# A six-layer cross network: a second Strassen level for product 4 in both tiles, result blocks in an idle state tile, one more residual by DMA, and another order of weight loads

## The chip, the cores and the metric

The kernel runs on one core of a Trainium2 chip. Its metric is the device time of one execution in microseconds (us), lower is better. Three runs of the kernel before took 2219.45, 2219.56 and 2220.05 us; the median is 2219.56 us.

A core has five engines that run at the same time, each with its own queue in order. PE (TensorE) multiplies matrices and leaves the sums in PSUM banks. ACT (ScalarE) and DVE (VectorE) work element by element; here ACT brings PSUM banks to SBUF, and DVE adds and multiplies tiles within SBUF. POOL (GpSimd) and SP (SyncE) mostly issue transfers, which 16 DMA engines carry out.

## The reference

The batch has 16384 rows of 1024 features in bfloat16, and there are six layers:

```python
x = x0
for l in range(6):
    proj = einsum('bd,de->be', x, ws[l]) + bs[l]
    x = x0 * proj + x
return x
```

Each layer is thus one 16384x1024 by 1024x1024 product, a bias, an elementwise product with the first input, and a residual (adding the x from before the layer).

## The kernel before, in words

**Tiles and units.** The batch is cut into 16 tiles of 1024 rows (the code calls one a pair, `pr`), and two tiles make a group, of which there are eight. A *unit* is one layer of one tile; the kernel runs 96 units, within a group layer by layer: tile one (lane 0), then tile two (lane 1) of layer 0, then both of layer 1, and so on. So two neighbouring units use the same weights, and a unit's result is wanted by the unit after next. x is held transposed, features on partitions. There are three x0 tiles and three state tiles (`xst`); a group uses two of each, so one state tile is idle most of the time.

**Products.** A unit's 1024x1024 by 1024x1024 product is cut into 2x2 blocks of 512 and done with seven block products in place of eight (Strassen's method in Winograd's form). The code calls them 1 to 7. T1 to T4 are differences of x blocks, made by DVE: T1 = B12 - B11, T2 = B22 - T1, T3 = B22 - B12, T4 = B21 - T2. Weight sums 5, 6, 7 and 3 are made once in the first group and kept in DRAM. With bias, the four result blocks are Q = P1 + P2, U = P1 + P6 + P5 + P3, V = P1 + P6 + P7 + P5 and W = P1 + P6 + P7 + P4.

A block product on one level (function `group`, line 313) is four groups `P4.0` to `P4.3` of four 128x512 matmuls. With a second level (function `inner`, line 490) it is seven inner products, `4p1` to `4p7`, of four 128x256 matmuls each. Products 5, 2 and 3 have a second level in nearly all units. Product 4 has it where `K4` (line 152) names the lane: in both lanes in layer 0, and in lane 1 alone in layers 1 to 4. Seven units are plain, with one level throughout: the six of the first tile and the very last unit.

On one level product 4 is added into the PSUM banks in which P1, P6 and P7 already stand, and ACT brings the sum out with the bias (`E4.m`) as W. On two levels it has its own banks: DVE prepares `4t13`, `4t2`, `4t4` from T4, ACT moves seven pieces (`4e_...`, `4f1`, `4f2`), DVE adds `4cc`, and then `Wa` adds V to it while V is still P1 + P6 + P7.

**End of a unit.** DVE adds the parts (`Q1`, `Ua`, `Ub`, `Wa`, `Va`), multiplies each block by x0 (`Qm`, `Um`, `Vm`, `Wm`, line 560) and adds the residual. In layers 1 to 4 the residual of the blocks Q, U and V is an accumulating DMA issued by POOL (line 563, named `Qx`, `Ux`, `Vx`), and that of W is a DVE addition, `Wx`; `DMA_RES` (line 153) says which. Block W is at block row 2, column 1 ("block 21").

**Buffers.** The parts and results are in seven `ev` tiles. `NEXT` (line 176) says which tile takes over which part from one unit to the next, so that a tile read by a late instruction isn't written too early.

**Weights.** Weight blocks of 512 KB go through a ring of 12 SBUF slots. In groups two to eight a layer loads 10 or 11 of them in a fixed sequence (line 225; "5i" is the set of quarter sums of block 5). A load is issued on SP when the oldest slot's last use is issued (`pump`, line 239), so it goes to the slot of the load 12 places before it.

**Order.** PE's order within a unit is written out by hand: `PE_TWO` (line 25) where products 5, 2 and 3 have a second level, `PE_FOUR` (line 29) where product 4 has it too. The other engines' order comes from a planner (`schedule`, line 51): with planned durations it computes for each operation the latest time that keeps PE from waiting, and on each engine the ready operation with the earliest such time goes next. The order is then fixed. `ACCUM` (line 40) is the time from issue to landing that it plans for a residual DMA.

Of the kernel before, what the change touches and what calls it, by code (L numbers as in the profile page):

```python
# [9 lines left out]
ADD = mybir.AluOpType.add  # L10
# [12 lines left out]
P3.0 P4.3 P4.1 P4.0 P4.2  # L23
""".split()
PE_TWO = """
5p5 P1.1 5p1 P1.0 P1.3 5p2 2p5 5p6 2p1 P1.2 5p3 2p2 5p7 2p6 P6.0 5p4 2p3 3p5 2p7 3p1 P6.1 2p4 3p2 3p6 P6.2 P6.3 3p3
3p7 P7.0 P7.1 P7.2 3p4 P7.3 P4.1 P4.0 P4.3 P4.2
""".split()
PE_FOUR = """
5p5 P1.0 5p1 2p5 2p1 P1.1 5p2 5p6 2p2 P1.2 2p6 P1.3 5p3 5p7 2p3 2p7 P6.0 3p5 5p4 2p4 P6.1 P6.3 3p1 4p5 P6.2 4p1 3p2  # L30
P7.0 4p2 3p6 4p6 P7.1 3p3 4p3 4p7 P7.2 3p7 4p4 P7.3 3p4
""".split()
PE_LAST = """
P1.0 P1.1 P1.2 P1.3 P2.0 P2.1 P2.2 P2.3 P5.0 P5.1 P5.2 P5.3 P6.0 P6.1 P6.2 P6.3 P3.0 P3.1 P3.2 P3.3 P7.0 P7.1 P7.2 P7.3
# [2 lines left out]
ARRIVE = {"rows0": 4.9, "w0.1": 6.4, "rows1": 8.9, "rows2": 11.3, "w0.2": 11.9, "h0": 14.3, "h1": 15.5, "q": 17.5, "next": 21.0, "raw1": 40.0}  # L37


ACCUM = 9.0  # L40


class Op:
# [85 lines left out]
def kernel(  # L129
# [7 lines left out]
    nc = tc.nc  # L137
    P = nc.NUM_PARTITIONS
# [10 lines left out]
    KQ, HQ, NQ = KH // 2, H // 2, NB // 2  # L149
    RING = 12  # L150
    NDUMMY = 8
    K4 = {0: (0, 1), 1: (1,), 2: (1,), 3: (1,), 4: (1,)}
    DMA_RES = {1: "QUV", 2: "QUV", 3: "QUV", 4: "QUV"}

    const = ctx.enter_context(tc.tile_pool(name="const", bufs=1))
    dram = ctx.enter_context(tc.tile_pool(name="dram", bufs=1, space=bass.MemoryType.DRAM))
# [16 lines left out]
    ip["4"] = ip["2"]  # L173
    P1s, P5s, Q, U, V, W, C3 = (work.tile([P, KH, KH, P], BF16, name=f"ev{i}") for i in range(7))
    EV = {"5c": P5s, "3c": C3, "U": U, "V": V, "W": W, "Q": Q, "P1s": P1s}
    NEXT = {"5c": "3c", "3c": "5c", "U": "W", "V": "U", "W": "V", "Q": "Q", "P1s": "P1s"}
    home = {r: r for r in EV}
    TURNED, rows = ((0, 0), (1, 0), (0, 1)), (P1s, U, V)
    zeros = tin["4"][:, 0]
    ident = const.tile([P, P], BF16, name="ident")  # L180
# [40 lines left out]
    for gl in range(NGROUP * L):  # L221
        if gl < L:
            ring_seq += [(gl, w, "load") for w in RAW] + [(gl, w, "make") for w in MADE]
        else:
            ring_seq += [(gl, w, "load") for w in "1 5 5i 2 2i 6 3 3i 7 4 4i".split()[:11 if gl % L in K4 else 10]]
    slot = {(gl, w): f"slot{i % RING}" for i, (gl, w, _) in enumerate(ring_seq)}
    wt, uses_left, live = {}, {}, []
    pos = {"next": 0}
# [49 lines left out]
    for u, (pr, l) in enumerate(units):  # L278
        one, first, last = plain(u), u == 0, u == NU - 1
        if not first:  # L280
            home = {r: home[NEXT[r]] for r in home}
        P1s, P5s, Q, U, V, W, C3 = (EV[home[r]] for r in ("P1s", "5c", "Q", "U", "V", "W", "3c"))
        CB = {"5": P5s, "2": Q, "3": C3, "4": W}
        gl, grp, lane = gl_of(u), pr // 2, pr % 2
        x0T, xst = x0Ts[pr % 3], xsts[pr % 3]
        xs = x0T if l == 0 else xst
        X0 = {q: f"x0.{pr % 3}.{q[0]}{q[1]}" for q in QD}
# [25 lines left out]
        def group(name, w, bank, bname, rhs, rname, m, start, gl=gl, kmajor=kmajor):  # L313
            def fn():
                for k in range(KH):
                    r = rhs[:, k, :] if kmajor else rhs[:, :, k, :]
                    o = bank[:] if kmajor else bank[:].rearrange("p (j r) -> p j r", r=P)
                    nc.tensor.matmul(o, lhsT=wt[(gl, w)][:, k, m * P:(m + 1) * P], rhs=r,  # L318
                                     start=(start and k == 0), stop=(k == KH - 1), skip_group_check=True)
            if first and name in ("P5.0", "P5.1"):  # L320
                rname = rname + ["w0.5a"]
            else:
                rname = rname + wname(w)
            pe(name, 0.863, fn, rname, [bname], [w], at={"1": ARRIVE["w0.1"], "2": ARRIVE["w0.2"]}.get(w, 0.0) if first else 0.0)
# [25 lines left out]
        def fence(q, sp, u=u):  # L350
            def fn():
                nc.gpsimd.dma_start(seen[:], x0Ts[sp][0:1, q[1], q[0] * KH, 0:32])
            op(f"fence@{u}", "POOL", 0.6, 0.6, fn, [f"x0.{sp}.{q[0]}{q[1]}"], ["xbar"])

        if l == 0 and lane == 1:
            for q in QD:
# [119 lines left out]
        if not one:  # L476
            for X, a, b in (("5", 0, 1), ("2", 2, 3), ("3", 0, 1), ("4", 2, 3))[:len(inn)]:
                Bm, src = SRC[X]
                C, pn = CB[X], Pn[X]
                if kmajor:  # L480
                    q = lambda dh, n, k, Bm=Bm: Bm[:, dh * KQ + k, n * NQ:(n + 1) * NQ]
                    tk = lambda i, k, X=X: tin[X].rearrange("p i (k b) -> p i k b", k=KQ)[:, i, k]
                else:
                    q = lambda dh, n, k, Bm=Bm: Bm[:, n * KQ:(n + 1) * KQ, dh * KQ + k, :]
                    tk = lambda i, k, X=X: tin[X].rearrange("p i (j k r) -> p i j k r", j=KQ, k=KQ)[:, i, :, k, :]
                c = lambda dh, n, C=C: C[:, n * KQ:(n + 1) * KQ, dh * KQ:(dh + 1) * KQ, :].rearrange("p j m r -> p m j r")
                cn = lambda dh, n, pn=pn: [pn(2 * dh) + f".{n}", pn(2 * dh + 1) + f".{n}"]
                call = [pn(m) for m in range(KH)]

                def inner(i, bank, start, X=X, gl=gl, q=q, tk=tk, src=src, kmajor=kmajor):  # L490
                    quad = {1: (0, 0), 2: (1, 0), 3: (1, 1)}
                    rhs = (lambda k: q(*quad[i], k)) if i in quad else (lambda k: tk({4: 3, 5: 0, 6: 2, 7: 1}[i], k))
                    rn = {1: src, 2: src, 3: src, 4: X + "t4", 5: X + "t13", 6: X + "t2", 7: X + "t13"}[i]
                    w = X if i in (1, 2, 4) else X + "i"

                    def fn():
                        if i in (1, 2, 4):
                            k0, e0 = {1: (0, 0), 2: (KQ, 0), 4: (KQ, HQ)}[i]
                            wv = wt[(gl, w)][:, k0:k0 + KQ, e0:e0 + HQ]
                        else:  # L500
                            wi = weight(gl, w) if gl < L else weight(gl, w)[:]
                            wv = wi.rearrange("p q (k e) -> p q k e", k=KQ)[:, {5: 0, 6: 1, 3: 2, 7: 3}[i]]
                        for m in range(KQ):
                            for k in range(KQ):
                                o = pX[bank][:, m * NQ:(m + 1) * NQ]
                                nc.tensor.matmul(o if kmajor else o.rearrange("p (j r) -> p j r", r=P), lhsT=wv[:, k, m * P:(m + 1) * P],  # L506
                                                 rhs=rhs(k), start=(start and m == 0 and k == 0), stop=(k == KQ - 1), skip_group_check=True)
                    if gl < L and w.endswith("i"):
                        dep, wl = [f"is.{w}.{({5: '5', 6: '6', 3: '3', 7: '7'})[i]}", ISN[w]], []
                    else:  # L510
                        dep, wl = ([] if X in "24" else wname(w)), [w]
                    pe(X + f"p{i}", 0.436, fn, [rn, Xn[bank]] + dep, [Xn[bank]], wl)

                v3 = lambda bank: pX[bank][:].rearrange("p (m j r) -> p m j r", m=KQ, r=P)
                inner(5, b, True)
                copy(X + "e_p5", ip[X][:].rearrange("p j (m r) -> p m j r", r=P), v3(b), [Xn[b]], [("2" if X == "4" else X) + "ps"])
                inner(1, a, True)
                copy(X + "f1", pX[b][:], pX[a][:], [Xn[a]], [Xn[b]])
                inner(2, b, False)
                copy(X + "e_c11", c(0, 0), v3(b), [Xn[b]], call)  # L520
                inner(6, a, False)
                copy(X + "f2", pX[b][:], pX[a][:], [Xn[a]], [Xn[b]])
                inner(3, b, False)
                copy(X + "e_u0", c(0, 1), v3(b), [Xn[b]], call)
                inner(7, a, False)
                copy(X + "e_u1", c(1, 1), v3(a), [Xn[a]], call)
                inner(4, a, False)
                copy(X + "e_c21", c(1, 0), v3(a), [Xn[a]], call)
                ch = C[:, KQ:KH].rearrange("p j (d m) r -> p d j (m r)", d=2)
                ttop(X + "cc", ch, ch, ip[X][:].unsqueeze(1).to_broadcast([P, 2, KQ, KQ * P]), ADD, [("2" if X == "4" else X) + "ps"] + call, call, n=1024)  # L530
# [16 lines left out]
        if not last:  # L547
            if not one:
                ttop("Q1", Q[:], Q[:], P1s[:], ADD, allm("Q") + allm("P1s"), allm("Q"))
            ttop("Ua", U[:], U[:], P5s[:], ADD, allm("U") + allm("5c"), allm("U"))  # L550
            if not one:
                ttop("Ub", U[:], U[:], C3[:], ADD, allm("U") + allm("3c"), allm("U"))
            if "4" in inn:
                ttop("Wa", W[:], W[:], V[:], ADD, allm("W") + allm("V"), allm("W"))
            ttop("Va", V[:], V[:], P5s[:], ADD, allm("V") + allm("5c"), allm("V"))
            for nm, C, q in (("Q", Q, (0, 0)), ("U", U, (0, 1)), ("V", V, (1, 1)), ("W", W, (1, 0))):
                if l == 0:
# [148 lines left out]
        load_half("4", h)  # L706
    nc.sync.dma_start_transpose(out=blk(x0Ts[0], 1, 1), in_=x0[NB:2 * NB, H:2 * H])

    held = [i for i in order if ops[i].name.startswith("ld") and ops[i].name.endswith(".1@1")]
    for i in held:  # L710
        ops[i].fn()
    for i in order:
        if i not in held:
            ops[i].fn()
        for k in ops[i].weights:
            if k in uses_left:
                uses_left[k] -= 1
        pump()
# [30 lines left out]
```

## Time and profile before

| what | value |
|---|---|
| median of three runs | 2219.56 us |
| the profiled execution, whole | 2219.68 us |
| its span, first to last instruction | 2217.9 us |
| granted TensorE clock | 0.999 |
| PE busy | 2208.2 us (100% of the span) |
| DVE busy | 2144.3 us (97%) |
| ACT busy | 2037.4 us (92%) |
| POOL busy | 204.9 us (9%) |
| moved by DMA | 478.66 MB, mean 216 GB/s |

Busy time counts overlapping instructions once. Neighbouring instructions of DVE and of ACT overlap at their edges in the records, so a group's mean duration is longer than the distance at which such instructions follow each other: three DVE additions of 128x2048 that stand in one line of the timeline take 3.49 us together, though each is recorded with 1.22 us. The share of DMA is the mean share of busy time of 16 engines by the time of their packets, which overlap too, so it can be above 1 in a stretch.

### The profile page before, as it was taken

What the parts mean: (1) busy time and instruction counts of PE and PEld (TensorE: products, weight loads), DVE (VectorE), ACT (ScalarE), POOL (GpSimd) and SP (SyncE); (2) the same over time, 40 slices, a digit from 0 to 9 for tenths busy, and PEclk for the clock granted to TensorE, in tenths of its full rate; (3) what the DMA queues carried; (4) which work ended last, traced back from release to release, by engine and by line L of the source; (5) the groups of instructions that cost most, each with busy time, mean ns of one, the idle gap of its engine ahead of it and who ended that gap; (6) DMA issues with size and microseconds to landing.
All of it is one profiled execution on the core that took longest, in us unless ns stands there. A gap on an engine that the chain in (4) does not pass through costs nothing.

```text
span 2217.9 us, 39582 instructions
## 1 busy us (share of the span) xinstructions
PE 2208.2 (100%) x14625; PEld 1427.9 (64%) x14625; DVE 2144.3 (97%) x2527; ACT 2037.4 (92%) x3642; POOL 204.9 (9%) x263
## 2 busy tenths in 40 slices
PE   9999999999999999999999999999999999999998
PEld 5555566666666666666666666666666666666664
DVE  8999999999999999999999999999999999999997
ACT  7888899999999999999999999999999999999997
POOL 1122100110001100011000110011100111001110
PEclk9999999999999999999999999999999999999999
DMA  8777899768996689866898679986799877997777
GB/s 256 207 203 208 201 226 258 190 172 209 259 257 179 173 227 252 256 176 177 228 254 244 171 193 233 265 214 177 207 225 256 217 180 224 224 251 196 200 224 166
DMA packets 454306, 478.66 MB, mean 216 GB/s; under 512 B 269024, under 2 KB 381152, under 8 KB 454112
## 3 DMA queue, kind: packets, MB, share of 16 engines
q1 hardware_dynamic: 418352, 349.49, 53.8%
q0 software_dynamic: 35168, 126.38, 28.2%
q8 instruction: 114, 1.87, 0.3%
q14 instruction: 80, 0.66, 0.1%
q10 hardware_dynamic: 592, 0.27, 0.0%
HBM read 252.72 MB, written 58.20 MB: 140 GB/s over the span
## 4 chain that ended last, share of the span: by engine, by line
PE 98%; DMA 0%; DVE 0%; SPq 0%; issue 0%; POOLq 0%; ACT 0%; DVEq 0%; ACTq 0%
PE pA L318 52%; PE pX L506 43%; PE pX L318 3%; DMA wp<-in_ws_dram 0%; SPq L690 0%; DVE ev L204 0%; DMA xst<-x0T 0%; SPq L697 0%; DVE x0T L204 0%; DVE T L204 0%; POOLq L744 0%; ACT ev L337 0%; DVE x0T L421 0%; SPq L703 0%; SPq L700 0%
## 5 line engine op out<-in xcount | busy, mean ns | idle before, releaser
L506 PEld LDWEIGHTS <-wp 128*128 128x128 bf16 x8424 | 824.2, 98 | 272.3 <-issue 1.0
L337 ACT ACTIVATE ev<-pA,b_all 128x512 bf16<-128x512 f32 x1291 | 883.2, 691 | 114.2 <-PE pA L318 73.7
L318 PE MATMUL pA<-T,wp 128*128 128x512 bf16 x3856 | 924.0, 379 | 0.0
L318 PEld LDWEIGHTS <-wp 128*128 128x128 bf16 x5728 | 560.2, 98 | 493.8 <-issue 2.5
L327 ACT CAST ev<-pX 128x512 bf16<-128x512 f32 x1284 | 700.5, 596 | 22.5 <-PE pX L506 15.0
L506 PE MATMUL pX<-ti,wp 128*128 128x256 bf16 x4748 | 658.0, 273 | 0.0
L204 DVE TENSOR_TENSOR ev<-ev,ev 128x2048 bf16<-128x2048 bf16 x419 | 501.5, 1213 | 44.4 <-ACT ev L327 36.9
L204 DVE TENSOR_TENSOR ev<-ev,x0T 128x2048 bf16<-128x2048 bf16 (+1 forms) x324 | 383.9, 1204 | 1.0
L327 ACT COPY pX<-pX 128x512 f32<-128x512 f32 x628 | 364.6, 593 | 3.6
L318 PE MATMUL pA<-xst,wp 128*128 128x512 bf16 x1280 | 319.5, 379 | 0.0
L563 POOL DMA_DIRECT2D xst<-ev x192 | 166.0, 866 | 1294.6 <-ACT ev L337 491.9
L506 PE MATMUL pX<-xst,wp 128*128 128x256 bf16 x1736 | 260.4, 273 | 0.0
L506 PE MATMUL pX<-T,wp 128*128 128x256 bf16 x1588 | 238.2, 273 | 0.0
L204 DVE TENSOR_TENSOR ev<-ev,ip 128x1024 bf16<-128x1024 bf16 x314 | 209.2, 683 | 0.0
L204 DVE TENSOR_TENSOR T<-xst,T 128x2048 bf16<-128x2048 bf16 x160 | 194.8, 1217 | 2.5 <-PE pX L506 1.6
L204 DVE TENSOR_TENSOR T<-xst 128x2048 bf16<-128x2048 bf16 x160 | 194.8, 1217 | 0.1
L327 ACT CAST ip<-pX 128x512 bf16<-128x512 f32 x314 | 184.8, 589 | 0.4 <-PE pX L506 0.4
L204 DVE TENSOR_TENSOR xst<-ev,xst 128x2048 bf16<-128x2048 bf16 x124 | 150.7, 1217 | 0.0
L204 DVE TENSOR_TENSOR ti<-T,ti 128x512 bf16<-128x512 bf16 x272 | 113.4, 417 | 0.1
L204 DVE TENSOR_TENSOR ti<-xst 128x1024 bf16<-128x1024 bf16 x148 | 101.4, 685 | 8.3 <-PE pX L506 7.8
L204 DVE TENSOR_TENSOR ti<-xst,ti 128x1024 bf16<-128x1024 bf16 x148 | 101.2, 684 | 0.1
L204 DVE TENSOR_TENSOR ti<-T 128x1024 bf16<-128x1024 bf16 x136 | 92.9, 683 | 0.0
(57 smaller groups left out, 698.9 us busy)
## 6 DMA issues: line engine op xcount, KB each, us to landing
wp<-Lc SPq DMA_DIRECT2D x329, 512.0 KB, 6.1
xst<-ev POOLq DMA_DIRECT2D x192, 512.0 KB, 5.1
wp<-in_ws_dram SPq DMA_DIRECT2D x148, 512.0 KB, 6.8
out_dram<-x0T SPq DMA_DIRECT2D x60, 512.0 KB, 4.3
Lc<-wp POOLq DMA_DIRECT2D x24, 512.0 KB, 6.0
Lc<-xst POOLq DMA_DIRECT2D x23, 512.0 KB, 5.3
ev<-in_x_dram SPq DMA_DIRECT2D x3, 512.0 KB, 6.2
wp<-in_ws_dram SPq DMA_DIRECT2D x4, 256.0 KB, 7.5
```

Source lines behind the costliest of these rows:

```text
L204: nc.vector.tensor_tensor(out=o, in0=a, in1=b, op=op)
L318: nc.tensor.matmul(o, lhsT=wt[(gl, w)][:, k, m * P:(m + 1) * P], rhs=r, start=(start and k == 0), stop=(k == KH - 1), skip_group_check=True)
L327: act(name, lambda: nc.scalar.copy(out=dst, in_=src), rd, wr)
L337: act(name, lambda: nc.scalar.activation(out=dst, in_=src, func=IDENT, bias=b_all[:, c:c + 1], scale=1.0), rd, wr, True)
L506: nc.tensor.matmul(o if kmajor else o.rearrange("p (j r) -> p j r", r=P), lhsT=wv[:, k, m * P:(m + 1) * P], rhs=rhs(k), start=(start and m ...
L563: nc.gpsimd.dma_start(xblk(xst, *q), C[:], accum_op=ADD)
```

## The change

1. `K4` names both lanes in layers 0 to 4, so lane 0 of layers 1 to 4 has a second level in product 4 too and runs by `PE_FOUR` (except the plain first tile).
2. `DMA_RES` names W too: all four residuals of layers 1 to 4 are accumulating DMAs. `ACCUM` is 9.5 in place of 9.0.
3. In groups two to eight, lane 1 of layers 1 to 4 puts Q, U, V and W into the four blocks of the idle state tile (`S` names) and not into `ev` tiles. `NEXT` is another one, and a dependence without an instruction (`lend`) keeps the idle tile's other users apart from it.
4. Weight loads go in another sequence (`LOAD_ORDER`), and `PE_TWO` and `PE_FOUR` are other orders.
5. `Ua` is listed after `Wa` and not before `Ub`, which sets the order among additions that the planner rates alike.

The first loads of the second tile's x0, which the code sends ahead of everything else, are sent as before; only the list's name is another. `pump` is as it was.

```diff
 PE_TWO = """
-5p5 P1.1 5p1 P1.0 P1.3 5p2 2p5 5p6 2p1 P1.2 5p3 2p2 5p7 2p6 P6.0 5p4 2p3 3p5 2p7 3p1 P6.1 2p4 3p2 3p6 P6.2 P6.3 3p3
-3p7 P7.0 P7.1 P7.2 3p4 P7.3 P4.1 P4.0 P4.3 P4.2
+5p1 2p5 5p5 P1.1 P1.0 5p6 2p1 5p2 P1.2 P1.3 5p3 2p2 5p7 2p6 P6.0 3p5 5p4 2p7 2p3 P6.1 3p1 P6.2 2p4 3p6 3p2 P7.0 P7.1
+P6.3 3p3 P7.2 3p7 P7.3 P4.0 P4.1 P4.3 3p4 P4.2
 PE_FOUR = """
-5p5 P1.0 5p1 2p5 2p1 P1.1 5p2 5p6 2p2 P1.2 2p6 P1.3 5p3 5p7 2p3 2p7 P6.0 3p5 5p4 2p4 P6.1 P6.3 3p1 4p5 P6.2 4p1 3p2
-P7.0 4p2 3p6 4p6 P7.1 3p3 4p3 4p7 P7.2 3p7 4p4 P7.3 3p4
+P1.1 5p5 5p1 2p5 P1.3 P1.0 5p2 2p1 5p6 P1.2 2p2 2p6 5p3 5p7 P6.0 2p3 3p5 2p7 P6.3 5p4 2p4 P6.2 3p1 P6.1 4p5 3p2 4p1
+3p6 P7.0 4p2 4p6 3p3 P7.1 4p3 3p7 4p7 P7.2 3p4 4p4 P7.3
...
-ACCUM = 9.0
+ACCUM = 9.5
+LOAD_ORDER = "1 5i 2i 5 2 6 3i 3 4i 4 7".split()
...
-    K4 = {0: (0, 1), 1: (1,), 2: (1,), 3: (1,), 4: (1,)}
-    DMA_RES = {1: "QUV", 2: "QUV", 3: "QUV", 4: "QUV"}
+    K4 = {l: (0, 1) for l in range(L - 1)}
+    DMA_RES = {l: "QUVW" for l in range(1, L - 1)}
...
-    NEXT = {"5c": "3c", "3c": "5c", "U": "W", "V": "U", "W": "V", "Q": "Q", "P1s": "P1s"}
-    home = {r: r for r in EV}
+    NEXT = {"5c": "3c", "3c": "Q", "U": "U", "V": "W", "W": "V", "Q": "5c", "P1s": "P1s"}
+    cycle = {r: r for r in EV}
+    home = cycle
...
-            ring_seq += [(gl, w, "load") for w in "1 5 5i 2 2i 6 3 3i 7 4 4i".split()[:11 if gl % L in K4 else 10]]
+            ring_seq += [(gl, w, "load") for w in LOAD_ORDER if w != "4i" or gl % L in K4]
...
-            home = {r: home[NEXT[r]] for r in home}
+            cycle = {r: cycle[NEXT[r]] for r in cycle}
+        gl, grp, lane = gl_of(u), pr // 2, pr % 2
+        idle = (2 * grp + 2) % 3
+        home = dict(cycle)
+        if grp > 0 and lane and 0 < l < L - 1:
+            home.update({r: "S" + r for r in "QUVW"})
+        EV.update({"S" + r: xsts[idle][:, i // 2, i % 2] for i, r in enumerate("QUVW")})
...
+        if grp > 0 and lane == 0 and l in (1, L - 1):
+            op(f"lend@{u}", "POOL", 0.0, 0.0, lambda: None, (), [f"S{r}.{m}" for r in "QUVW" for m in range(KH)] + [f"xs.{idle}.{a}{b}" for a, b in QD])
...
-            ttop("Ua", U[:], U[:], P5s[:], ADD, allm("U") + allm("5c"), allm("U"))
             if not one:
                 ttop("Ub", U[:], U[:], C3[:], ADD, allm("U") + allm("3c"), allm("U"))
             if "4" in inn:
                 ttop("Wa", W[:], W[:], V[:], ADD, allm("W") + allm("V"), allm("W"))
+            ttop("Ua", U[:], U[:], P5s[:], ADD, allm("U") + allm("5c"), allm("U"))
             ttop("Va", V[:], V[:], P5s[:], ADD, allm("V") + allm("5c"), allm("V"))
```

More of the change, by code (lines that the diff above doesn't have):

```diff
@@ L280 @@
         if not first:
-            home = {r: home[NEXT[r]] for r in home}
+            cycle = {r: cycle[NEXT[r]] for r in cycle}
[5 more added lines that the diff above has]
+        EV.update({"S" + r: xsts[idle][:, i // 2, i % 2] for i, r in enumerate("QUVW")})
         P1s, P5s, Q, U, V, W, C3 = (EV[home[r]] for r in ("P1s", "5c", "Q", "U", "V", "W", "3c"))
         CB = {"5": P5s, "2": Q, "3": C3, "4": W}
-        gl, grp, lane = gl_of(u), pr // 2, pr % 2
         x0T, xst = x0Ts[pr % 3], xsts[pr % 3]
@@ L318, in fn @@
                     nc.tensor.matmul(o, lhsT=wt[(gl, w)][:, k, m * P:(m + 1) * P], rhs=r,
-                                     start=(start and k == 0), stop=(k == KH - 1), skip_group_check=True)
+                                                    start=(start and k == 0), stop=(k == KH - 1), skip_group_check=True)
             if first and name in ("P5.0", "P5.1"):
@@ L505, in fn @@
                                 o = pX[bank][:, m * NQ:(m + 1) * NQ]
-                                nc.tensor.matmul(o if kmajor else o.rearrange("p (j r) -> p j r", r=P), lhsT=wv[:, k, m * P:(m + 1) * P],
-                                                 rhs=rhs(k), start=(start and m == 0 and k == 0), stop=(k == KQ - 1), skip_group_check=True)
+                                nc.tensor.matmul(
+                                    o if kmajor else o.rearrange("p (j r) -> p j r", r=P), lhsT=wv[:, k, m * P:(m + 1) * P],
+                                    rhs=rhs(k), start=(start and m == 0 and k == 0), stop=(k == KQ - 1), skip_group_check=True)
                     if gl < L and w.endswith("i"):
@@ L707 @@
     nc.sync.dma_start_transpose(out=blk(x0Ts[0], 1, 1), in_=x0[NB:2 * NB, H:2 * H])
-    held = [i for i in order if ops[i].name.startswith("ld") and ops[i].name.endswith(".1@1")]
-    for i in held:
+    early = [i for i in order if ops[i].name.startswith("ld") and ops[i].name.endswith(".1@1")]
+    for i in early:
         ops[i].fn()
     for i in order:
-        if i not in held:
+        if i not in early:
             ops[i].fn()
```

## The prediction, made before the changed kernel ran

> **What bounds the kernel now.** I read the page first (engines, the chain that ended last, the DMA queues), then what PE waited for, then busy time unit by unit.
>
> ```profile
> PE 2208.2 (100%) x14625; PEld 1427.9 (64%) x14625; DVE 2144.3 (97%) x2527; ACT 2037.4 (92%) x3642; POOL 204.9 (9%) x263
> ...
> q0 software_dynamic: 35168, 126.38, 28.2%
> ...
> PE 98%; DMA 0%; DVE 0%; SPq 0%; issue 0%; POOLq 0%; ACT 0%; DVEq 0%; ACTq 0%
> ```
>
> PE is the bound, with DVE only 64 us of busy time behind. The view of waits, for PE:
>
> ```profile
> PE pX L681 <- DVE ti L678: 1.2, 1, 1.2
> PE pX L318 <- ACT pX L327: 0.7, 2, 0.5
> PE pX L318 <- DVE T L204: 0.6, 1, 0.6
> PE pX L417 <- DVE x0T L421: 0.4, 1, 0.4
> ```
>
> That is 2.9 us in all, so nothing but less PE work shortens the kernel. Next the busy times of stretches cut at unit borders of the fifth group: start and end, length, then PE, PEld, DVE, ACT, POOL, clock, DMA share, GB/s.
>
> ```profile
> 1135.60:1158.19 22.59, 22.59 (x163) 15.67 (x161) 22.59 (x29) 21.88 (x41) 0.00 (x0) 1.00 1.02 248
> 1158.19:1181.17 22.98, 22.98 (x151) 14.47 (x149) 22.98 (x28) 21.29 (x38) 1.42 (x2) 1.00 1.09 289
> ...
> 1249.33:1272.31 22.98, 22.98 (x151) 14.49 (x149) 21.72 (x26) 21.11 (x38) 2.59 (x3) 1.00 0.64 167
> 1272.31:1294.90 22.59, 22.59 (x162) 15.66 (x161) 22.14 (x28) 21.63 (x41) 2.59 (x3) 1.00 0.81 226
> ...
> 1363.45:1386.43 22.98, 22.98 (x150) 14.49 (x149) 22.98 (x27) 21.05 (x38) 0.00 (x0) 1.00 1.09 248
> ```
>
> Rows: layer 0 lane 1, layer 1 lane 0, layer 3 lanes 0 and 1, layer 5 lane 1. A unit costs PE 22.98 us with product 4 on one level, 22.59 on two. DVE is full from layer 5 through layer 1 lane 0, and PE goes on: a full DVE with work ready is borne. In layer 3 it idles 1.26 + 0.45 = 1.71 us a pair of units.
>
> **The gain on PE.** Lane 0 of layers 1 to 4 changes shape in seven groups (the first tile is plain): 28 units at 22.98 - 22.59 = 0.39 us, 10.9 us. It lies wholly on the path that sets the end. The chain in order of time gives the same from its pieces (start, length, matmuls):
>
> ```profile
> 1255.55 1.75 PE pX L506 x16
> ...
> 1268.14 4.32 PE pA L318 x20
> ```
>
> Product 4 on one level is 16 matmuls at 4.32 / 20, 3.46 us; on two, 28 at 1.75 / 16, 3.06 us. A group of four is 0.864, an inner product 0.437.
>
> **DVE.** Distances come from the timeline:
>
> ```profile
> 1254.54 3.49 DVE L204 TENSOR_TENSOR ev<-ev,x0T 128x2048 bf16<-128x2048 bf16 x3
> ```
>
> Less the last one's 1.22 us, 128x2048 operations start 1.14 apart; by the starts, 128x1024 ones are 0.60 apart, 128x512 ones 0.33. Lane 0 gains `4t13` 0.60, `4t2` and `4t4` 0.33 each, `4cc` 0.60, `Wa` 1.14: 3.00 us. Both lanes lose `Wx`, 2.28 a pair. A pair goes from 43.86 busy (21.72 + 22.14) to 44.58, while PE goes from 45.57 to 45.18: spare time falls from 1.71 to 0.60. Over the kernel: 28 x 3.00 - 64 x 1.14 = +11 us, DVE 2155. Layer 0 has this shape in both lanes already, DVE full, and PE didn't stop. I cost it at nothing but for one place. Its cover is those 0.60 us; every further us of idle that the order forces on DVE in a pair lengthens 28 pairs.
>
> **The one place: T2 in lane 0.** In the changed order of DVE the border from lane 1 to lane 0 in layers 2 to 4 reads 3cc, 4cc, Ub, Wa, 3t13, Ua, 23t2, Va, T2; T2 stands behind Va, and `P6.0` needs T2. Counted from the new unit's start: the old unit ends with P7.2, 3p4, 4p4, P7.3 so P7.2 ends at -1.74. ACT takes it up some 0.20 later (a group issued from 1267.98 on, over at 1268.84, is evicted from 1269.04), then the two copies 0.59 and 0.49 further on: -0.95 and -0.46. These rows give the step from ACT to a waiting DVE:
>
> ```profile
> 1262.22 1.10 ACT L327 CAST ev<-pX 128x512 bf16<-128x512 f32 x2
> ...
> 1263.36 1.23 DVE L204 TENSOR_TENSOR ev<-ev,ev 128x2048 bf16<-128x2048 bf16 x1 [1.26 <-ACT ev L327]
> ```
>
> The second cast starts near 1262.73 and DVE at 1263.36: 0.63. So 3cc starts at -0.32, 4cc at 0.28, Ub 0.88, Wa 2.02, 3t13 3.16, Ua 3.76, 23t2 4.90, Va 5.50, T2 6.64; T2 is out at 7.86, or 7.91 with the 0.04 to 0.05 of such a hand-over. In PE's new order four groups and ten inner products stand ahead of `P6.0`: 7.83. PE would wait 0.03 to 0.08, say 0.07, in 20 units (three a group, two in the first that has them): 1.4 us. From both sides: nothing if a hand-over is 0.1 shorter, 8 us if the chain comes 0.4 later in each. I take 1.4, since all its steps have rows here. Other users have room: T2 of lane 1 stands ahead of Ua, 23t2 is done 0.9 before 2p6.
>
> **ACT.** Four biased evictions (0.59 apart) become seven copies (0.48): about +1 us in lane 0, so 21.11 becomes the 21.65 of today's lane 1, in 22.59. Layer 0 runs two such units in a row without a wait. Nothing.
>
> **POOL and the fourth residual.** 64 more issues of 0.86 us: POOL goes from 2.59 to 3.45 us a unit, queueing only more residuals and, in the first group, saves of weight sums. There, 8 more DMAs stand between saves, and DVE is 1.14 a unit shorter; PE has no wait, so no gain: nothing. The landing matters: `2t13` of the unit after next needs W, and DVE is queued behind it. DVE work between a block's multiplication and its next reader, by the distances above: U 9.3 and 10.4 us (behind lane 1 and lane 0), W 9.1 and 9.9, V about 10, Q more. Landings of this transfer in the whole run, least, median, most:
>
> ```profile
> DMA to landing us min/median/max: 4.5/5.1/9.5
> ```
>
> In layer 3 the most is 5.0 in the lane-0 stretch and 7.7 in the lane-1 stretch. Queue q0 is 28.2% of 2217.9 us, 625 us of all engines, for 239 transfers of 512 KB: 2.6 us each. One more a unit raises the share by 0.115: 0.64 to 0.75, 0.81 to 0.93, still below the 1.02 to 1.09 of layers 5 to 1, where weights land in 8.6 at the most. Bounds for the longest landing: 5.0 and 9.5; I take 8.5 for the lane-1 stretch (nearest row 7.7 at 0.81), under its 9.9. Nothing.
>
> POOL's issues here take 852 to 1191 ns, median 862, beside a DVE that is 97% busy; none was held for the length of a DVE operation. A rule of the Trainium skill speaks against the step all the same: SBUF — State Buffer, "SBUF: two separate sides", has it that POOL can't write the descriptors of its DMAs while DVE runs an operation in a two-port performance mode. By that rule each issue could wait for the end of a DVE operation, 1.22 us, and a landing of 8.5 would become 9.7, just under the 9.9: the sum stays, and the room is gone.
>
> **Buffers and weights.** Lane 1 writes its blocks to the idle state tile, which the previous group's outputs leave during layer 0; its first writer is lane 1 of layer 1, over 20 us later. Elsewhere `NEXT` makes 2's first result wait for Va of lane 1: Va is out at 6.72, the result could leave its bank at 6.71. That is a wait of ACT's, and the next inner product that needs the bank, 2p3, starts at 8.69: nothing. Weight loads: from the last use of a slot's old block to the first use of the new one the least is 12.6 us in the new order (block 5, into layer 5) against 9.6 before (3i); landings have a median of 6.4 and a worst of 11.6. The order of loads is worth nothing, in either direction.
>
> **The sum.** Against the profiled execution: 2219.68 - 10.9 + 1.4 = 2210.2 us; the median of the three runs is 0.12 lower, so 2210.1.
>
> **Rivals.**
> 1. *Small waits eat part of it.* DVE's or ACT's late operations hold PE a further 0.1 to 0.3 us a pair: 28 x 0.1 to 0.3 = 3 to 8 us on top of the sum, so 2213 to 2218.5. For: the first unit of layer 0 (1386.43 to 1409.17) is 22.74 long, not 22.59, without a releaser shown. Against: 2.9 us of waits today.
> 2. *DVE becomes the bound* (the other side). If the 1.71 us of idle in a pair are forced by the order and stay, a pair takes 44.58 + 1.71 = 46.29, against 45.57 before: +0.72 x 28 = 20 us, 2240. It decides from 45.57 - 44.58 = 0.99 us of forced idle on. For: 1.26 of it is a wait for ACT at one place in lane 0. Against: that unit is the light one, and DVE has no idle at all over the four full units. By my own chain 0.5 us a unit before 3cc is left, which is about the spare time and no more.
> 3. *The fourth residual lands late*, by rising traffic or because DVE holds up POOL's issues. DVE then waits in `2t13` or T1. A wait up to 0.60 us a pair is free; from 0.99 on, a landing of some 10.9 us in lane 1's stretch, it is slower than before; 12 us would give 2.1 a pair: (44.58 + 2.1 - 45.57) x 28 = +31, 2251. Against: 7.7 now, and issues of at most 1.19 us. The second of the two ways is the rule of that page, SBUF — State Buffer, in the Trainium skill.
>
> **How the numbers follow.** Three runs lie within 0.03%; I call 0.2%, 4.4 us, the least that can be told from no change: faster is below 2215.1, slower above 2224.0. Forecast 0.62, its own range 2207.6 to 2213 (layer 0's 0.15 us waits gone as well and no T2 wait, up to twice the T2 wait and a little more). Rival 1: 0.14, 0.06 of it faster. Rival 2: 0.14, 0.02 of it within 0.2%. Rival 3: 0.10, slower (0.08 by traffic, 0.02 by held issues). Faster 0.62 + 0.06 = 0.68, same 0.08 + 0.02 = 0.10, slower 0.12 + 0.10 = 0.22. The range takes the forecast, rival 1 and the mild end of rival 2: 2207.6 to 2224, some 0.8.
>
> **What would show it.** Right: lane 0 of layers 2 to 4 takes 22.6 to 22.7 us, PE's waits stay under 5 us and name T or DVE, DVE is some 2155 busy, 256 residuals land in under 9. Wrong: PE's waits come to tens of us in layers 1 to 4, DVE idle there names ACT (rival 2) or the residual's DMA (rival 3).

## The result, and the profile after

The changed kernel takes 2283.25 us (median of five runs, 2282.85 to 2284.88); the kernel before, run beside it, 2220.05 us. The ratio is 1.0288 with a 95% interval of 1.0277 to 1.0299: 63 us slower, where 10 us faster was forecast. The profiled execution has a span of 2281.5 us, against 2217.9 before.

The page of the kernel after, its busy times, its queue of accumulating DMAs (packets, MB, share of the 16 engines) and its chain that ended last:

```profile
PE 2209.3 (97%) x14913; PEld 1459.7 (64%) x14961; DVE 2165.2 (95%) x2603; ACT 2054.4 (90%) x3726; POOL 256.6 (11%) x327
...
q0 software_dynamic: 44384, 159.94, 34.1%
...
PE 41%; DVE 37%; DMA 14%; issue 6%; ACT 1%; SPq 0%; DVEq 0%; POOLq 0%; ACTq 0%
```

PE was 98% of the chain before; now DVE and DMA have half of it, though DVE's busy time is only 10 us above the forecast (2165 against 2155). The view of waits, for PE and then for DVE (total us, times, longest us):

```profile
PE pX L516 <- ACT pX L334: 23.7, 29, 2.1
PE pA L325 <- DVE T L206: 13.3, 17, 0.8
PE pX L516 <- DVE ti L206: 10.6, 13, 1.2
```

```profile
DVE ti L206 <- DMA xst<-ev: 40.9, 27, 4.6
DVE ti L206 <- DMA x0T<-in_x_dram: 16.8, 6, 4.1
DVE ev L206 <- ACT ev L344: 12.0, 10, 2.6
```

PE's waits went from 2.9 to over 50 us, and name ACT and DVE. By place, the row for `T` is T2 in front of `P6.0`, and the row for `ti` is `23t2` in front of `2p6`; all but one of these 30 waits stand in lane 0 of layers 2 to 4. Of the 23.7 us for ACT, 21 stand in the first unit of layer 0 and the first of layer 5. But DVE itself waits 40.9 us for residuals (`xst<-ev`; line 574 now) and 16.8 us for loads of the next group's x0. The landing times of the residuals say why; least, median, most, in the kernel after:

```profile
DMA to landing us min/median/max: 4.5/6.6/13.0
```

The most was 9.5 before. Where the time went, from the distances between the first evictions of P1 in neighbouring units (a unit of this shape takes 22.59 us of PE work; where the order of products ahead of that eviction has changed, its 0.44 us are taken out):

| place | us |
|---|---|
| 28 units with less PE work | -10.9 |
| lane 0 of layers 2 to 4 (22.59 to 26.56 each), seven groups | +34.5 |
| first unit of layer 0 (25.60 to 26.05 in place of 22.74), six groups | +19.4 |
| from lane 1 of layer 4 to the next group, six groups | +11.5 |
| last units and tail | +7.0 |
| first group | +1.8 |
| the rest of layers 0 and 1 | +0.4 |
| sum | +63.7 |

Lane 1 of layers 1 to 3 takes exactly 22.59 everywhere. So most of the loss has two addresses: lane 0 in the middle layers, and the border from layer 4 into the next group.

**Lane 0 in the middle layers.** Windows of the kernel after cut at unit borders of the fifth group (columns as in the prediction): layer 2 lane 1, layer 3 lanes 0 and 1.

```profile
1253.49:1276.08 22.59, 22.59 (x162) 15.66 (x161) 19.64 (x22) 21.76 (x40) 3.44 (x4) 1.00 0.72 187
1276.08:1301.82 25.74, 23.23 (x162) 15.63 (x161) 25.24 (x33) 21.83 (x40) 3.44 (x4) 1.00 0.88 225
1301.82:1324.41 22.59, 22.59 (x162) 15.65 (x161) 20.48 (x24) 21.76 (x41) 3.44 (x4) 1.00 0.71 186
```

DVE idles about 3 us at the end of the lane-1 stretch, and the lane-0 unit is 3.15 longer. The timeline of DVE at that border (start, length, operation, and in brackets the idle time before it and what ended it):

```profile
1276.30 0.69 DVE L206 TENSOR_TENSOR ti<-xst 128x1024 bf16<-128x1024 bf16 x1 [3.04 <-DMA xst<-ev]
...
1278.98 1.22 DVE L206 TENSOR_TENSOR xst<-xst,ev 128x2048 bf16<-128x2048 bf16 x1
1280.11 1.22 DVE L206 TENSOR_TENSOR xst<-xst 128x2048 bf16<-128x2048 bf16 x1
1281.25 0.68 DVE L206 TENSOR_TENSOR ti<-xst 128x1024 bf16<-128x1024 bf16 x1
...
1283.59 1.22 DVE L206 TENSOR_TENSOR xst<-xst,ev 128x2048 bf16<-128x2048 bf16 x1
1284.72 1.22 DVE L206 TENSOR_TENSOR T<-xst,T 128x2048 bf16<-128x2048 bf16 x1
```

The first row is `2t13`, which stood 3.04 us for W's residual. Behind it, in order, come 3cc and 4cc (left out), Ub, Wa, `3t13`, Ua and 23t2 (left out), Va, T2: the border that the prediction wrote down, but all of it late. The chain in order of time goes on from T2 (start, us, what):

```profile
1268.53 11.49 DMA xst<-ev
...
1284.72 1.23 DVE T L206
1285.95 0.04 issue
1285.99 1.02 PE pA L325 x4
```

PE's `P6.0` starts 0.04 after T2. The 11.49 us piece is V's residual, which lands at 1280.01. `3t13` reads it at 1281.25 and doesn't wait, since W's wait has put it back already; 3.04 earlier it would have stood 1.8 us for V. In the pair before, `3t13` stood 1.33 us for V.

**What else moved.** The DMAs of this lane-1 stretch, by time from its first eviction of P1, set beside the same stretch of the kernel before:

| | before | after |
|---|---|---|
| weight loads | 11, issued from 5.64 to 22.07 | 11, issued from 5.20 to 21.77 |
| residuals near them (time issued, us to landing) | U 3.84, 8.0; Q 14.29, 6.8 | U 7.82, 7.9; W 10.09, 12.6; V 15.03, 11.5; Q 18.37, 12.0 |
| these transfers of 512 KB, and time until all have landed | 13 in 25.0 us | 15 in 30.7 us |
| lane 0's V | issued at 2.01, landed after 4.9 | as above |

U, W and V are lane 0's, Q is lane 1's. So not one but two residuals joined the loads here: W, which was a DVE addition, and V, which was sent 3.6 us ahead of the first load and is now sent 9.8 us behind it. The loads are issued over the same length of time. Over lane 1 of layers 2 and 3 in groups two to eight, the 13 transfers take 24.7 to 27.0 us before, the 15 take 28.5 to 31.4 after.

The mean share of DMA over such a unit hides the burst. The stretch for which the prediction read 0.81 (layer 3 lane 1 before), cut where U is issued:

```profile
1272.31:1277.65 5.34, 5.34 (x40) 3.81 (x39) 5.34 (x7) 4.96 (x10) 0.87 (x2) 1.00 0.11 21
1277.65:1294.90 17.25, 17.25 (x124) 11.85 (x122) 16.80 (x22) 16.67 (x32) 1.72 (x2) 1.00 1.03 290
```

It is 0.11 for 5 us and 1.03 for 17. So in its burst the kernel before already had a share as high as in the layers with the highest (1.02 to 1.09).

### The profile page after: what moved, and what is told of

It reads as the page before. It is cut to its first block, busy times and chain, and to the rows that moved or that the text cites. A ratio compares the mean times of both kernels' runs of the same rounds, so it can differ in the third digit from the quotient of the medians.

```text
span 2281.5 us, 40476 instructions
## 1 busy us (share of the span) xinstructions
PE 2209.3 (97%) x14913; PEld 1459.7 (64%) x14961; DVE 2165.2 (95%) x2603; ACT 2054.4 (90%) x3726; POOL 256.6 (11%) x327
## 4 chain that ended last, share of the span: by engine, by line
PE 41%; DVE 37%; DMA 14%; issue 6%; ACT 1%; SPq 0%; DVEq 0%; POOLq 0%; ACTq 0%
PE pA L325 21%; PE pX L516 18%; DVE ev L206 14%; DMA xst<-ev 12%; DVE ti L206 9%; DVE T L206 8%; DVE xst L206 6%; PE pX L325 2%; DMA x0T<-in_x_dram 1%; DMA wp<-Lc 0%; DVE wp L206 0%; ACT ev L344 0%; ACT pX L334 0%; DMA xst<-x0T 0%; SPq L701 0%
## 5 line engine op out<-in xcount | busy, mean ns | idle before, releaser
L325 PE MATMUL pA<-T,wp 128*128 128x512 bf16 x3377 | 851.7, 380 | 15.0 <-DVE T L206 13.3
L516 PE MATMUL pX<-ti,wp 128*128 128x256 bf16 x5196 | 725.1, 273 | 16.0 <-DVE ti L206 10.6
L344 ACT ACTIVATE ev<-pA,b_all 128x512 bf16<-128x512 f32 x955 | 649.6, 691 | 83.9 <-PE pA L325 46.6
L206 DVE TENSOR_TENSOR ev<-ev,ev 128x2048 bf16<-128x2048 bf16 (+1 forms) x307 | 367.6, 1219 | 12.7 <-ACT ev L344 12.0
L516 PE MATMUL pX<-T,wp 128*128 128x256 bf16 x1924 | 289.1, 273 | 8.0 <-ACT pX L334 7.8
L206 DVE TENSOR_TENSOR ev<-ev,x0T 128x2048 bf16<-128x2048 bf16 (+1 forms) x212 | 253.5, 1204 | 1.1
L574 POOL DMA_DIRECT2D xst<-ev x144 | 124.3, 863 | 759.9 <-ACT ev L334 412.2
L344 ACT ACTIVATE xst<-pA,b_all 128x512 bf16<-128x512 f32 x224 | 154.7, 691 | 9.4
L574 POOL DMA_DIRECT2D xst<-xst x112 | 96.2, 859 | 571.7 <-ACT ev L334 356.3
L206 DVE TENSOR_TENSOR ti<-xst 128x1024 bf16<-128x1024 bf16 x148 | 102.1, 691 | 46.1 <-DMA xst<-ev 40.9
L206 DVE TENSOR_TENSOR xst<-xst,x0T 128x2048 bf16<-128x2048 bf16 x112 | 136.9, 1223 | 0.7
```

The source lines that it names most:

```text
L206: nc.vector.tensor_tensor(out=o, in0=a, in1=b, op=op)
L344: act(name, lambda: nc.scalar.activation(out=dst, in_=src, func=IDENT, bias=b_all[:, c:c + 1], scale=1.0), rd, wr, True)
L574: nc.gpsimd.dma_start(xblk(xst, *q), C[:], accum_op=ADD)
```

## The experiments

My theory A: the residuals land late because too many transfers meet in lane 1's stretch, and DVE's wait for them delays PE through T2 and `23t2`. Its rival B: DVE's order and its load (prediction's rival 2) are the bound, and the DMA waits only show where DVE's idle time falls. For the border of groups, theory C: layer 4 as changed sends V too late, and the x0 loads hang behind it.

**All residuals a quarter of the size.**

```diff
-nc.gpsimd.dma_start(xblk(xst, *q), C[:], accum_op=ADD)
+nc.gpsimd.dma_start(xblk(xst, *q)[:, 0:1], C[:, 0:1], accum_op=ADD)
```

> The changed kernel with every residual DMA of layers 1 to 4 cut to a quarter of its block (one of four row tiles, 128 KB in place of 512); three quarters of those residuals are left out, all orders and waits stay. Theory A (residuals that land late behind the weight loads of lane 1 hold DVE, and that holds PE): landings under 6 us, lane 0 of layers 2 to 4 back to 22.6 us each, and the time falls by the 30 us or so that these units cost, to 2235 to 2255 if the first unit of layer 0 stays long (its x0 loads come late for another reason) and to 2210 to 2215 if it goes too. Theory B (the order of DVE and ACT itself forces idle, whatever the DMAs do): the waits stay, 2270 or more.

2239.79 us, ratio 1.0088 (1.0072 to 1.0105): 43 us of the 63 are gone. Lane 0 of layers 1 to 4 takes 22.59 to 22.62 in groups two to eight, the first unit of layer 0 still 25.80 to 26.05 from the third group on. The waits of DVE in this kernel:

```profile
DVE ti L206 <- DMA x0T<-in_x_dram: 18.0, 7, 4.8
DVE ev L206 <- ACT ev L344: 15.1, 10, 3.7
```

No row names a residual, and its DVE does the same work in the same order. B is refuted, A holds, and the wait for x0 is a matter of its own.

**W's residual alone a quarter of the size.**

```diff
-nc.gpsimd.dma_start(xblk(xst, *q), C[:], accum_op=ADD)
+p = slice(0, 1 if nm == "W" else KH)
+nc.gpsimd.dma_start(xblk(xst, *q)[:, p], C[:, p], accum_op=ADD)
```

> The changed kernel with W's residual DMA alone at a quarter of its size (three quarters of W's residual in layers 1 to 4 are left out); Q, U and V are whole, all orders stay. That is the bytes of six and a half residuals a pair. Theory A, by count: V and Q land in 7 to 9 us, most units of lane 0 in layers 2 to 4 take 22.6, and what is left is the late x0 loads: 2238 to 2250. Theory A, by place (V of lane 0 and Q of lane 1 were moved among the loads): they still take 10 us and more, 2255 to 2275.

2240.36 us, ratio 1.0094 (1.0079 to 1.0109): the same 43 us, from one transfer in four. In layers 2 to 4 V then lands in 8 to 10 us, Q in 9 to 10, W itself in 6 to 9, and lane 0 is at 22.59 nearly everywhere. DVE's rows:

```profile
DVE ti L206 <- DMA x0T<-in_x_dram: 20.4, 9, 4.9
...
DVE ti L206 <- DMA xst<-ev: 5.5, 2, 5.3
```

So landings of up to 10 us were nearly free in these layers, and many of the 9 to 13 us in the kernel after were not; the covers worked out in the prediction (9.1 to 10.4) put the step there.

**W's addition on DVE again.**

```diff
-DMA_RES = {l: "QUVW" for l in range(1, L - 1)}
+DMA_RES = {l: "QUV" for l in range(1, L - 1)}
```

> The changed kernel with W's residual back on DVE in all layers: product 4 on two levels in both lanes, three residuals by DMA. Theory A: with six residual DMAs a pair in place of eight their landings in lane 1's stretch fall to 9 us and less, but DVE has 44.6 + 2.3 = 46.9 us of work for a pair on which PE spends 45.2, so DVE bounds layers 1 to 4, with no wait for a residual's DMA to speak of: 2235 to 2260. Theory B: 2283 or more.

2260.21 us, ratio 1.0178 (1.0163 to 1.0194). Lane 0's V lands in 5 to 10 us (median 8.3), lane 1's Q mostly in 4.6. The page of this kernel, and its waits of PE and of DVE:

```profile
PE 2210.0 (98%) x14913; PEld 1459.3 (65%) x14961; DVE 2221.4 (98%) x2667; ACT 2059.2 (91%) x3726; POOL 202.1 (9%) x263
```

```profile
PE pA L325 <- DVE T L206: 15.8, 14, 1.5
PE pX L516 <- ACT pX L334: 14.1, 27, 0.8
```

```profile
DVE ti L206 <- DMA xst<-ev: 1.2, 1, 1.2
```

The residuals hold next to nothing, but DVE has 56 us more to do than after, and now bounds by itself: from the third group on it has no idle time in layers 0 to 4, and its 2221 us busy are more than the kernel before takes. With the second level in lane 0, W's addition has no good place: on DVE it makes DVE the bound, as a DMA it makes the landings late.

**The fourth residual on the kernel before.** Here `K4`, buffers and loads stay as they were, and the other engines' order is planned anew.

```diff
-DMA_RES = {1: "QUV", 2: "QUV", 3: "QUV", 4: "QUV"}
+DMA_RES = {l: "QUVW" for l in range(1, L - 1)}
```

> The kernel before with nothing changed but W's residual by DMA, product 4 and all orders as they were. Theory A, by count: the fourth transfer fills the DMA engines, residuals of lane 1's stretch land in 10 us and more, and the time rises by 10 us or more, 2230 and above. Theory A, by place: it is where in the unit a residual is issued that matters; here Q, U and V keep their places, only W itself lands in 8 to 10 us, and DVE has 1.1 us a unit more to spare: 2217 to 2224. Theory B: 2218 to 2221.

2231.79 us, ratio 1.0053 (1.0038 to 1.0068). DVE has 2.28 us a pair less to do, and the kernel is 12 us slower. Waits of its DVE:

```profile
DVE T L204 <- DMA xst<-ev: 19.6, 27, 2.5
DVE ti L204 <- DMA xst<-ev: 11.6, 8, 2.5
```

Lane 1's Q lands in 9 to 10.5 us, lane 0's U mostly in 8.4 to 10.8, W in 4.5 to 6.7. The fourth residual costs time by itself, less than in the changed kernel: here V is still sent ahead of the loads (6.2 us to landing in the fifth group). How much of the 12 us is the landings' was not separated: 3 of them are lost in the last units and the tail, and in the order planned anew DVE's waits for ACT grew as well, from 42 to 83 us.

**The second level taken back, all else changed.**

```diff
-K4 = {l: (0, 1) for l in range(L - 1)}
+K4 = {0: (0, 1), 1: (1,), 2: (1,), 3: (1,), 4: (1,)}
```

> The changed kernel with product 4 on one level in lane 0 of layers 1 to 4 as before; four residuals by DMA, the idle state tile, the new load order and the new unit orders stay. Theory A: the DMA engines are as full as in the changed kernel, residuals of lane 1's stretch take 10 us and more, but DVE has 3 us a pair less to do and can stand more of a wait; the late x0 loads remain or grow milder: 2235 to 2270, slower than before although the second level is gone. If the second level itself is the cause: 2218 to 2224.

2258.13 us, ratio 1.0175 (1.016 to 1.019), with Q in 10 to 11.9 us, V in 8.5 to 10.5. So the second level isn't needed for a loss; but by place it is another loss. DVE stands 37 us for residuals here, nearly as long as in the kernel after, and yet lane 0 of layers 2 and 3 loses only 3 us in all seven groups, against 17 in the kernel after with its gain taken off. DVE has 3.00 us a pair less to do here, room for such waits; the planned order differs too, so the share of each is not shown. The rest, of 39 us in the profiled execution, lies at layer 4 (9), between it and the next group (12), in lane 0 of layers 0 and 1 (6), at the end (8) and in the first group (1). PE's longest waits name DVE's additions in `xst` (20.1 us, 19 of them in lane 0 of layers 4 and 5); why was not taken apart.

**Layer 4 as before.**

```diff
-K4 = {l: (0, 1) for l in range(L - 1)}
-DMA_RES = {l: "QUVW" for l in range(1, L - 1)}
+K4 = {0: (0, 1), 1: (0, 1), 2: (0, 1), 3: (0, 1), 4: (1,)}
+DMA_RES = {1: "QUVW", 2: "QUVW", 3: "QUVW", 4: "QUV"}
```

> The changed kernel with layer 4 alone as it was: one level of product 4 in lane 0, three residuals by DMA. Theory C, for the first unit of layer 0 (26.05 us in place of 22.74): the x0 loads of the next group wait for the last residual of layer 4, which is V and now issued 10 us later, so they land late. It expects that unit to go back to under 23.5 us in seven groups, some 20 us, and with layer 4's own waits gone some 10 more, less 3 us of lost gain: 2250 to 2262. If the x0 loads are late from traffic alone, that unit stays over 25 us: 2270 to 2280.

2238.03 us, ratio 1.008 (1.0064 to 1.0097), better than expected. The first unit of layer 0 takes 22.62 in all seven groups: C holds; traffic alone isn't the cause, since with quarter-size residuals that unit stayed at 25.80 to 26.05. In the kernel after, lane 1 of layer 4 in the fifth group sends V 37.81 us after the unit's first eviction, before it was 30.33; the tiny transfer `let`, which waits for that landing, comes at 43.78 and not at 35.63; and the eight x0 loads that go with it run until 77.5 us and not 71.9. `3t13` of the next group's first unit needs one of them, which lands at 68.3 and not at 56.7; it stood 2.76 us for it. Whether the second level or W's transfer in layer 4 makes V late wasn't separated cleanly: with W on DVE everywhere the first two units of layer 0 take 48.9 us together, as in the kernel after (48.7), which points to the second level, but there DVE is the bound. So does the run before this one, with W by DMA and lane 0 on one level: V is sent at 35.5, and `3t13` waits for no x0 block in groups three to eight. Lane 0 of layers 2 and 3 gains too (+1.4 and +6.1 us in all remain of +10.4 and +12.1); how a change in layer 4 reaches them wasn't followed.

**Both together.** Quarter-size residuals and layer 4 as before.

> The changed kernel with the residual DMAs at a quarter of their size (three quarters of these residuals left out) and layer 4 as before. Theories A and C together, if they are all there is and add up: both losses go, the gain of 21 units (8 us) stays, less 2 us in the first group and 3 to 5 at the end that the runs so far show beside them: 2214 to 2219. A third cause of size would leave it above 2225.

2219.08 us, ratio 0.9996 (0.9987 to 1.0006), and groups two to seven take 272.4 to 272.5 us each, PE's work to 0.2 us; PE's whole list of waits:

```profile
PE pX L692 <- DVE ti L689: 1.2, 1, 1.2
PE pX L325 <- ACT pX L334: 0.7, 2, 0.5
PE pX L325 <- DVE T L206: 0.6, 1, 0.6
PE pX L325 <- ACT ev L344: 0.2, 1, 0.2
```

A and C account for nearly everything inside the groups. What is left of the expected gain is lost in the first group (1.5 us) and at the end (some 5); the end wasn't settled. A version that leaves out most of the residuals is thus only as fast as the kernel before.

**Order of the loads, two ways.** In the kernel after the old sequence, in the kernel before the new one:

```diff
-LOAD_ORDER = "1 5i 2i 5 2 6 3i 3 4i 4 7".split()
+LOAD_ORDER = "1 5 5i 2 2i 6 3 3i 7 4 4i".split()
```

> The changed kernel with the old sequence of weight loads. Theory A in the form that the new sequence bunches the loads: landings back to 8 or 9 us and a time below 2250. Theory A in the form that four residuals are too much for the stretch of lane 1 in any sequence: within 10 us of 2283. Theory B: 2283 within 3 us.

> The kernel before with the new sequence of weight loads and nothing else. It was worth about 10 us to the bad in the changed kernel. If that is the sequence itself, it shows here too, 2222 to 2230; if it needs the full DMA engines of the changed kernel, 2219 to 2221.

2272.85 us, ratio 1.0239 (1.0223 to 1.0254), and 2219.67 us, ratio 0.9999 (0.999 to 1.0009). The sequence is worth nothing while the transfers are hidden and 10 us when they aren't; the landings of V (9.4 to 12.4) and Q (9.5 to 12.9) stay what they were, so it isn't the cause.

**Telling the planner the truth.** `ACCUM` by block: 12 us for lane 0's V and W and lane 1's Q, 8.6 for lane 0's U, 6.5 for the others.

> The changed kernel with the planner told what it measured: 12 us for W and V of lane 0 and Q of lane 1, 8.6 for U of lane 0, 6.5 for the others, in place of 9.5 for all. Theory A: DVE's order then has work ahead of the late blocks, the waits of lane 0 in layers 2 to 4 go or become a few tenths each, and the time falls by 25 to 50 us, to 2233 to 2258; the rest stays because there isn't enough other work. Theory B: no better than 2275.

2255.87 us, ratio 1.0161 (1.0146 to 1.0176). Lane 0 goes down to 22.6 to 24.4, lane 1 up to 23.19, the first unit of layer 0 down to 23.60. The landings of V and Q hardly change (9.4 to 11.9); lane 0's U rises to a median of 10, its W falls to 7. Planned waits cost a little over half of the unplanned ones; what remains, 36 us, no order that this planner found takes away.

**Loads held back.** A transfer of 64 bytes on POOL's queue behind Q's residual reads weight block 2, so that loads into its slot and later ones should come after the burst; and then the same in layers 1 to 3, with layer 4 as before and three residuals by DMA in the first group:

```diff
+nc.gpsimd.dma_start(held[:], wt[(gl, "2")][0:1, 0, 0:32])
```

> The changed kernel with one tiny transfer added in lane 1 of layers 1 to 4 of groups two to eight: behind Q's residual on POOL it reads 64 bytes of weight block 2, so the slot of block 2 comes free only when Q has landed, and the seven loads from block 6 on wait for it. No transfer of size is taken away. Theory A, by place (the loads and the residuals of one stretch get in each other's way): V, W and Q land in 5 to 8 us, lane 0 of layers 2 to 4 is back near 22.6, and the time falls by some 35 us, to 2240 to 2255. Theory A, by count (there is too much traffic in all): the waits move to the weights, 2275 and above.

> The changed kernel with the loads held in layers 1 to 3, layer 4 as before, and three residuals by DMA in the first group. Theories A and C together: the waits of both are gone, 8 us of gain are left, less 3 to 5 at the end: 2213 to 2219, at least no slower than the kernel before. If holding the loads only moves the waits: 2235 and above.

2280.74 us, ratio 1.0282 (1.0266 to 1.0297), and 2244.35 us, ratio 1.0108 (1.0091 to 1.0125): both misses. Only the last four loads were held, not seven, so the first kernel did not put its question. V, W and Q still take 8 to 12 us, and the residuals of the quiet stretch rose, as the median of `xst<-xst` shows, here in the DMA issues of the first of the two kernels (KB, median us to landing):

```profile
xst<-xst POOLq DMA_DIRECT2D x112, 512.0 KB, 9.2
```

In the kernel after it reads 5.5. In the second kernel PE waits for weights too:

```profile
PE pA L326 <- DMA wp<-Lc: 8.9, 7, 3.5
```

The waits in good part only moved. No version that computes all of the function came out ahead of the kernel before.

## Why the prediction was wrong

**The gain on PE: right.** 22.59 us is the length of lane 0 wherever nothing holds it (with small residuals, in every lane 0 of layers 2 to 4), so 0.39 us a unit and 10.9 in all are there, and are eaten.

**T2 in lane 0: wrong, harmlessly.** The 1.4 us did not come: with small residuals no lane-0 unit of the middle layers waits for T2. The chain's price hung on less than 0.1 us. The place was the right one all the same, since `P6.0` waiting for T2 is where late residuals reach PE.

**DVE: right in kind.** 2165 us busy against 2155, and its order forces no idle that costs time (rival 2 falls with the quarter-size residuals). But 0.60 us of spare time a pair left nothing to absorb a late landing; that limit the prediction had written down. With DVE late, the room of the other users went too: where the prediction has "23t2 is done 0.9 before 2p6", PE waited 10.6 us in 13 places.

**The fourth residual, the step that failed:** "One more a unit raises the share by 0.115: 0.64 to 0.75, 0.81 to 0.93 [...] I take 8.5 for the lane-1 stretch (nearest row 7.7 at 0.81), under its 9.9. Nothing." In groups two to eight lane 0's W lands after 8.0 to 12.7 us (median 9.4), its V after 9.3 to 12.3 (10.7) and lane 1's Q after 9.7 to 13.0 (11.3), and DVE stood 40.9 us for W and V where "nothing" was forecast; it is rival 3, at a chance of 0.10. Three things are wrong in it. The share is a mean over a unit, while the loads and the residuals stand in one burst of 17 us in it, in which the share was 1.03 already, not "still below". The number to add was two, not one: V's issue moved from ahead of the loads into their midst, and only W was counted. And the upper bound of 9.5 was taken from the kernel before, where no unit sent so many transfers; a cover of 9.9 was thus never in danger within my own range. In hindsight the trace of before allowed a better estimate: 13 transfers took 25.0 us, so 15 take 28.8 (they took 30.7), and since the transfers are issued over no longer a time, the later ones land 3.8 us later than the 6.8 to 8.0 of before: 10.6 to 11.8.

**Rival 3's price: of the right size for its part.** It gave 2251, +31 with the gain already taken off, for a landing of 12 us in 28 pairs. The lane-0 loss less the gain is 34.5 - 10.9 = 23.6 us, from 21 pairs and landings of 9 to 13.

**Va and the buffers: "nothing" held only while DVE was on time.** ACT stood 31 us in 23 waits for Va of lane 1, the wait that the prediction put at 0.01 us, and none with small residuals. PE lost some 3 us by it in layers 2 and 3.

**x0 loads and layer 5: not in the prediction at all.** I didn't follow V of layer 4 to `let` and on to the x0 loads, which gives some 20 us in the first units of layer 0 and part of the 11.5 before it. A moved residual has a second reader there, and I priced only the first.

**Order of loads "worth nothing, in either direction":** right for the kernel before, off by 10 us in the changed one, where the DMA engines have no room. **First group "nothing":** 1.8 us. **POOL's issues:** 0.85 to 0.91 us, none held, so the second way of rival 3 didn't happen. The rule of the Trainium skill (SBUF — State Buffer, "SBUF: two separate sides") is about DVE operations in a two-port performance mode; the prediction applied it to the TENSOR_TENSOR operations of this kernel, for which neither the rule as quoted nor any run shows such a mode. The longest issue of a residual in any run took 1.21 us against a median of 0.86, so no hold of a whole DVE operation, 1.22 us, is seen.

## What to carry to other kernels

Judge an added transfer by the burst into which it falls, and by every transfer that the new order moves there with it: count the transfers from the first to the last of the burst, and set their time against the time between issue and reader, block by block. A mean share of DMA over a stretch can be 0.8 and the engines still be full for most of it. Work taken from a full engine and handed to DMA is not free when its reader stands in that engine's own queue: then a late landing stops the engine that it should have relieved.

## What the runs showed of the hardware

An accumulating transfer of 512 KB within SBUF lands after 4.5 us at the least, 4.5 to 6.3 us in a quiet stretch (lane 1's U, V and W in layers 1 to 3), and 8 to 13 us among weight loads (W, V and Q), where V and Q mostly land 3.8 us apart. A mixture of weight loads and such residuals moved 13 x 0.524 MB in 25.0 us, 273 GB/s, before, and 15 in 30.7 us, 256 GB/s, after: more transfers in the burst brought no more bytes in a second. The Trainium skill, in DMA: Bandwidth & Descriptors, "Anatomy of one DMA — SWDGE (gpsimd) path", has a fit of 2.0 us plus the bytes at 436 GB/s; by it such a transfer would take an estimated 3.2 us, and the least of this case is 4.5. A quarter of the size (128 KB) still takes 2.6 us at the least and 5.0 at the median for `xst<-ev`, yet in the kernel with only W cut down it freed the others.

Also unexpected: the times of the two effects don't add. The quarter-size residuals save 43 us and layer 4 as before 45, of 63 in all. So each saves some of what the other does: by place, layer 4 as before also takes 16 us off lane 0 of layers 2 to 4, and the quarter-size residuals take 5 off the border after layer 4. Why was not followed.
